# First weights converted by halves, last tokens of a pair stored in one transfer, and a new hand-written order, in an attention and MLP kernel on one core

## The chip, the core and the metric

One NeuronCore of a Trainium2 chip runs the whole program. The metric is the device time of one execution in microseconds (us); smaller is better. TensorE (PE) multiplies matrices, VectorE (DVE), ScalarE (ACT) and GpSimd (POOL) work element by element, and SyncE (SP) issues every transfer (DMA) of this kernel. Each engine takes its own instructions in order.

## The reference, cut to what matters

There are 8 batches (b) of 8 heads, 576 tokens, head size 64, and 32 memories. Softmax weights of `phi` over the tokens compress `k` and `v` to 32 rows per head; each token then attends to these 32 rows; and the result, 4608 tokens by 512 channels, goes through a two-layer MLP with a gate.

```python
a = np.exp(phi - np.max(phi, axis=2, keepdims=True))
a = a / (np.sum(a, axis=2, keepdims=True) + 1e-09)
k_m, v_m = einsum('bhsm,bhsd->bhmd', a, k), einsum('bhsm,bhsd->bhmd', a, v)
attn = softmax(scale * q @ k_m.T)           # over the 32 memories
x = (attn @ v_m) laid out as [4608, 512]
h = x @ w_in                                # 512 x 2048
g = h * np.clip(h + 3.0, 0.0, 6.0) / 6.0
out = g @ w_out                             # 2048 x 512
```

## The kernel before, in words

The program is a list of words, `ORDER`, which `play` turns into instructions one after the other. The order of the words is the order of the instructions on each engine, and the order of the transfers on SP's one queue. Nothing is reordered afterwards; an instruction waits only for its data, for its buffer, and for what stands before it on its engine.

The weights arrive as 64-bit floats and are converted on the chip, once, among the first batches' work. `w_in` comes in 8 units, `w_out` in 8 units too (1 MB each). For a unit u of `w_out` the words are `raw2.u` (load, L189), `ab.1.u` (ACT, size of the number, L198), `cl.1.u` and `sh.1.u` (DVE, clamp and shift, L206 and L209), `ro.1.u` (ACT, the low word, L202), `si.1.u` (DVE, sign, L214), `to.1.u` (DVE, sum, L225), `sx.u` (ACT, high part, L232) and `sy.u` (POOL, low part, L236). The units of `w_in` go the same way under `raw.u.k`, `ab.0.u.k` and so on; their loads, `ab`, `ro`, `si` and `to` are already by halves (k = 0, 1), `cl` and `sh` are whole.

A batch's attention part is `pt` (load of phi), `mx`, `xp`, `tr`, `pc` (exponentials by rows), `kvm.b.t` (memories from five loads `kv.b.t`), `nr`, `nk`, `tp`, `tk`, `sc`, `ct`, `cm`, `cs`, `ex`, `ds`, `dr`, `dm`, `bt`, `bh`, `bl` (the attention weights in two halves of 288 tokens). `fo` multiplies the memories into a unit of `w_in`. A slot is one batch and one tile of 128 of the 2048 channels: `g` (first product, L492), `u`, `m` (gate, L505, L508), `k`, `h`, `l` (parts, L512, L516, L519) and `a` (second product, L528). Batches 0 and 1 go through their slots twice (6 and 8 tiles first, kept in DRAM), the other six once, with 16 tiles each. `wm` (L614) is a product on a constant whose result nobody reads; the order has 60 of them.

Of a batch's 576 tokens, 512 are stored by `store` (L561). The last 64 tokens of two batches (a pair) are gathered and go through `rh`, `rl`, `ra` (L574, L577, L584) together; `re` (L597, L599) writes them to a tile of 128 rows, and `ro2` stores the tile: `rest_store` (L601 to L604) writes rows 0 to 63 behind the first batch of the pair, rows 64 to 127 behind the second. `ro2.3` is the last word of the program.

Of the kernel before, what the change touches and what calls it, by code (L numbers as in the profile page):

```python
# [45 lines left out]

WHOLE = 2
# [10 lines left out]
ct.0.0 kv.1.3 cm.0.0 cs.0.1 fo.0.0 xp.1.1 wm.25 ab.0.1.0 cs.0.0 vh.0.0 ex.0.1 wm.19 wm.22 kv.1.4 wm.7 wm.57 wm.26
wm.48 tr.1.0 wm.31 wm.58 ds.0.1 tr.1.1 raw2.1 wm.36 ex.0.0 xp.1.2 dr.0.1 tr.1.2 pc.1.0 dm.0.1 ds.0.0 wm.39 pc.1.2
wm.40 wm.23 wm.43 ab.0.1.1 kvm.1.0 wm.13 ro.0.1.1 pc.1.1 raw.5.0 kvm.1.1 dr.0.0 kvm.1.2 dm.0.0 cl.0.1 bt.0.1 sh.0.1  # L60
wm.49 ro.0.1.0 g.0.1 kvm.1.3 si.0.1.0 bt.0.0 raw.2.1 kvm.1.4 nr.1 g.0.0 to.0.1.0 si.0.1.1 bh.0.1 nk.1 bl.0.1 g.1.1
wm.24 g.1.0 ab.1.1 to.0.1.1 wm.17 wm.50 wm.42 wm.44 wm.55 cl.1.1 sh.1.1 u.0 ro.1.1 m.0 u.1 q.1.1 si.1.1 h.0 fo.0.1 l.0
wm.21 wm.54 wm.8 wm.0 wm.34 bh.0.0 raw.2.0 vh.0.1 m.1 vl.0.1 k.1 bl.0.0 to.1.1 ab.0.2.0 ab.0.2.1 cl.0.2 a.0.0 sh.0.2
si.0.2.1 raw2.2 tp.1 tk.1 k.0 g.2 raw.3.0 sc.1.1 ro.0.2.1 wm.1 h.1 ro.0.2.0 u.2 ab.1.2 ct.1.1 a.0.1 wm.28 wm.12 g.3
si.0.2.0 to.0.2.0 l.1 q.1.0 cm.1.1 to.0.2.1 u.3 ab.0.3.0 wm.16 a.0.2 m.2 m.3 raw2.3 cl.1.2 ro.1.2 h.2 sx.1 wk.0 l.2
raw.3.1 sh.1.2 wm.47 a.0.3 sc.1.0 cs.1.1 fo.0.2 vh.0.2 sy.1 raw2.4 ex.1.1 ct.1.0 a.1 vl.0.2 wk.1 k.3 ab.0.3.1 cm.1.0
ds.1.1 h.3 cs.1.0 fo.1.0 vh.1.0 k.2 vl.1.0 si.1.2 ro.0.3.1 ro.1.3 pt.2 raw.5.1 to.1.2 g.4 a.2 ex.1.0 cl.0.3 l.3
ab.0.5.0 sx.2 ab.1.3 u.4 ds.1.0 dr.1.0 m.4 g.5 raw2.6 raw.4.0 a.3 u.5 sy.2 h.4 ab.0.5.1 m.5 q.2.1 dr.1.1 h.5 dm.1.0
fo.1.1 dm.1.1 l.4 fo.1.2 ro.0.5.0 bt.1.0 k.5 l.5 a.4 raw2.5 bh.1.0 vh.1.1 vh.1.2 bt.1.1 a.5.0 a.5.1 bl.1.0 bh.1.1
bl.1.1 mx.2 pn.2 vl.1.1 vl.1.2 g.6 sh.0.3 k.4 a.5.2 cl.0.5 si.0.3.0 ro.0.5.1 g.7 e.0.0 ro.0.3.0 u.6 to.0.3.0 m.6 e.0.1  # L70
si.0.3.1 mo.2 eo.0.0 h.6 to.0.3.1 a.5.3 u.7 k.6 raw.4.1 l.6 g.8 a.6.0 ro.1.4 m.7 raw.7.1 g.9 e.0.3 cl.1.3 u.8 sp.2
a.6.1 a.6.2 sh.0.5 e.0.2 m.8 g.10 h.7 k.7 ab.0.4.0 eo.0.1 a.6.3 k.8 l.7 u.9 si.0.5.0 ro.0.4.0 ab.0.4.1 m.9 si.0.5.1
to.0.5.0 raw.6.0 k.9 h.9 cl.0.4 l.9 sh.0.4 si.0.4.1 fo.1.3 a.7 vh.1.3 vl.1.3 u.10 to.0.5.1 h.8 ab.1.4 g.11 l.8 m.10
si.0.4.0 a.8 h.10 u.11 l.10 wk.2 m.11 cl.1.4 g.12 sh.1.3 to.0.4.0 k.10 u.12 ro.1.5 si.1.3 a.9 q.2.0 to.1.3 sh.1.4 wk.5
# [84 lines left out]
def attention_ffn_kernel(ctx: ExitStack, tc: tile.TileContext, pn, pt, kv, kl, qt, w1, w2, out):  # L159
# [547 lines left out]
```

## Time and profile before

| | |
|---|---|
| runs timed | 702.39 us (median of 3; 702.25, 702.39, 703.63) |
| the profiled execution | 701.81 us, of which the profile's span is 699.8 us |
| PE busy | 686.5 us (98% of the span), 5330 matmuls |
| DVE, ACT, POOL busy | 385.2, 325.3, 81.8 us |
| DMA moved | 98.10 MB, mean 140 GB/s |

PE is the engine to look at: what it does not do in its 98% is a little over 13 us, at the two ends for the most part. The other engines matter where PE waits for them. Times inside the profile count from the start of its span.

### The profile page before, as it was taken

The page shows a single profiled execution, that of the slowest core. Times are in us where ns is not written, and L with a number is a line of the kernel's source. Part 1 is how long each engine was busy: PE and PEld are TensorE (multiplying, and loading weights), DVE is VectorE, ACT ScalarE, POOL GpSimd, SP SyncE. Part 2 cuts the span into 40 slices and gives each one's busy share as a digit, 9 for nine tenths or more (in the row PEclk, how much of TensorE's full clock was granted, in tenths as well). Part 3 has the DMA queues.
Part 4 walks back from the last instruction along what each step waited for, and adds up shares of the span by engine and source line. Part 5 has one row for each costly group of instructions (what it writes and reads, how often), then busy time and mean ns, then how long its engine had stood idle before and what let it go on. Part 6 is the DMA issues. An engine that isn't in the chain of part 4 may idle for free. (4 is left out here: it accounts for less than half of the span.)

```text
span 699.8 us, 12717 instructions
## 1 busy us (share of the span) xinstructions
PE 686.5 (98%) x5330; PEld 579.4 (83%) x5330; DVE 385.2 (55%) x596; ACT 325.3 (46%) x635; POOL 81.8 (12%) x60
## 2 busy tenths in 40 slices
PE   6999999999999999999999999999999999999997
PEld 5778878888788888988878887888878888798885
DVE  5999989855744336633555434833355434652331
ACT  5787677545434343643344443544334433363340
POOL 0344020310400004000130001200021000400000
PEclk9999999999999999999999999999999999999999
DMA  9995837243415605540145431514038040410002
GB/s 360 410 417 207 297 119 268 94 140 121 133 61 182 267 1 154 187 166 1 66 159 185 143 122 55 221 62 155 0 145 281 2 151 1 136 61 1 1 0 76
DMA packets 28761, 98.10 MB, mean 140 GB/s; under 512 B 3104, under 2 KB 3872, under 8 KB 27680
## 3 DMA queue, kind: packets, MB, share of 16 engines
q1 hardware_dynamic: 28704, 97.29, 38.4%
q8 instruction: 42, 0.69, 0.4%
q14 instruction: 15, 0.12, 0.0%
HBM read 81.54 MB, written 15.73 MB: 139 GB/s over the span
## 5 line engine op out<-in xcount | busy, mean ns | idle before, releaser
L528 PE MATMUL acc<-w,parts 128*128 128x512 f32 x1536 | 379.0, 392 | 0.1
L528 PEld LDWEIGHTS acc<-w,parts 128*128 128x128 f32 x1536 | 279.6, 188 | 61.1 <-issue 7.7
L508 DVE SCALAR_TENSOR_TENSOR gf<-gf,ph 128x576 f32<-128x576 f32 x128 | 95.4, 751 | 173.4 <-ACT gf L505 172.8
L492 PE MATMUL ph<-phi,both 128*128 128x288 f32 x1008 | 173.1, 293 | 1.0 <-DVE both L471 0.8
L505 ACT ACTIVATE gf<-ph,three 128x576 f32<-128x576 f32 x128 | 94.5, 742 | 171.1 <-PE ph L492 138.3
L492 PEld LDWEIGHTS ph<-phi,both 128*128 128x128 f32 x1008 | 152.2, 188 | 12.3 <-issue 2.1
L519 DVE TENSOR_TENSOR parts<-gf,parts 128x512 fp32r<-128x512 f32 x128 | 90.2, 711 | 40.6 <-ACT parts L516 40.0
L492 PE MATMUL ph<-plo,both 128*128 128x288 f32 x504 | 108.1, 296 | 0.0
L516 ACT CAST parts<-gf 128x512 fp32r<-128x512 f32 x128 | 78.9, 619 | 62.0 <-DVE gf L508 30.6
L492 PEld LDWEIGHTS ph<-plo,both 128*128 128x128 f32 x504 | 80.3, 188 | 0.0
L415 POOL TENSOR_TENSOR st<-st,mx 128x576 f32<-128x576 f32 x15 | 18.3, 1228 | 401.3 <-DVE mx L411 398.4
L471 DVE TENSOR_TENSOR both<-pv,both 128x512 fp32r<-128x512 f32 x63 | 41.6, 680 | 23.2 <-ACT both L467 23.2
L584 PE MATMUL acc<-w,parts 128*128 128x512 f32 x192 | 46.3, 391 | 0.0
L467 ACT CAST both<-pv 128x512 fp32r<-128x512 f32 x63 | 35.5, 589 | 20.9 <-PE pv L454 18.4
L584 PEld LDWEIGHTS acc<-w,parts 128*128 128x128 f32 x192 | 35.6, 188 | 8.0 <-ACT o L550 0.4
L512 ACT COPY rest<-gf 128x64 f32<-128x64 f32 x128 | 30.0, 242 | 18.5 <-DVE gf L508 18.4
L454 PE MATMUL pv<-w,kvT 64*32 64x256 f32 x1024 | 32.5, 380 | 0.9 <-DMA w<-w_kept 0.9
L236 POOL TENSOR_TENSOR w<-tmp,w 128x1024 fp32r<-128x1024 f32 x8 | 20.7, 2583 | 90.7 <-ACT w L232 60.5
L454 PEld LDWEIGHTS pv<-w,kvT 64*32 64x32 f32 x1024 | 18.0, 106 | 12.6 <-issue 3.2
L440 POOL TENSOR_TENSOR plo<-pT,phi 128x576 fp32r<-128x576 f32 x16 | 23.9, 1499 | 15.6 <-ACT phi L435 15.3
L418 ACT ACTIVATE st<-st 128x576 f32<-128x576 f32 x16 | 10.9, 686 | 30.3 <-POOL st L415 30.1
L614 PE MATMUL acc<-rest,ident 128*128 128x128 f32 x120 | 19.7, 301 | 1.6 <-DVE rest L660 1.6
(61 smaller groups left out, 391.9 us busy)
## 6 DMA issues: line engine op xcount, KB each, us to landing
w<-w_kept SPq DMA_DIRECT2D x48, 512.0 KB, 6.3
kvt<-in_kv SPq DMA_DIRECT2D x32, 516.0 KB, 6.8
qh<-in_qt SPq DMA_DIRECT2D x16, 576.0 KB, 10.1
raw<-in_w SPq DMA_DIRECT2D x8, 1024.0 KB, 7.6
raw<-in_w SPq DMA_DIRECT2D x16, 512.0 KB, 9.7
out_t<-o SPq DMA_DIRECT2D x16, 512.0 KB, 3.5
ptile<-in_pt SPq DMA_DIRECT2D x8, 576.0 KB, 4.1
w_kept<-w SPq DMA_DIRECT2D x8, 512.0 KB, 4.3
```

Of the source, the lines that this page charges most:

```text
L440: nc.gpsimd.tensor_tensor(plo, self.pT[hf], probs[self.b, hf][0].bitcast(F32), ALU.subtract)
L454: nc.tensor.matmul(self.pv[u][j * M : (j + 1) * M, g], self.kvT[rows, g, j * M : (j + 1) * M], chunk[rows, j, :].bitcast(F32), start=True, ...
L467: nc.scalar.copy(both[:, 0], self.pv[u])
L471: nc.vector.tensor_tensor(both[:, 1], self.pv[u], both[:, 0].bitcast(F32), ALU.subtract)
L492: nc.tensor.matmul(self.ph[:, hf], w[:, g, fs], x[:, g * HALF : (g + 1) * HALF], start=(i == 0), stop=(i == len(seq) - 1),)
L505: nc.scalar.activation(self.halves(), self.ph, AF.Relu, bias=three)
L508: nc.vector.scalar_tensor_tensor(self.halves(), self.halves(), 6.0, self.ph, ALU.min, ALU.mult)
L512: nc.scalar.copy(rest[:, self.f, at : at + REST], self.gf[:, MAIN:])
L516: nc.scalar.copy(self.parts[:, 0], self.gf[:, :MAIN])
L519: nc.vector.tensor_tensor(self.parts[:, 1], self.gf[:, :MAIN], self.parts[:, 0].bitcast(F32), ALU.subtract)
L528: nc.tensor.matmul(accs[self.run, t], self.parts[:, k, t * P : (t + 1) * P], w, start=self.first and i == 0, stop=self.last and i == 2,)
L584: nc.tensor.matmul(accs["rest", self.p], self.parts[:, i // 2, t * P : (t + 1) * P], w2_parts(4 * self.r + t)[i % 2], start=self.r == 0 an ...
```

## The change

Three things change.

1. `load_w2`, `clamp` and `shift` take a half k, and `w_out` is laid out in DRAM with the two halves of a unit one after the other. For units 0, 1 and 2 each of `raw2`, `ab`, `cl`, `sh`, `ro`, `si` and `to` becomes two words, one for each half. Units 3 to 7 stay whole; their load now reads two runs per partition instead of one.
2. `rest_store` issues one transfer instead of two: `out` is viewed as batches by tokens by channels, and the two batches' last 64 tokens are one pattern of 2 x 64 rows on the DRAM side; on the SBUF side stands the tile of 128 rows. There are four such stores.
3. The first half of `ORDER`, up to about slot 36, is written anew; the later half is the same word for word. The number of `wm` words stays 60.

```diff
-    def load_w2(u):
-        part = wpool.tile([P, UNIT], I64, name=f"raw2_{u}", tag=f"w2_{u}")
-        nc.sync.dma_start(out=part, in_=w2[u])
-        raw[1, u] = {0: (slice(0, UNIT), *words(part))}
+    raw_w2 = {}
+
+    def load_w2(u, k=None):
+        if u not in raw_w2:
+            raw_w2[u] = wpool.tile([P, UNIT], I64, name=f"raw2_{u}", tag=f"w2_{u}")
+        n = UNIT // 2
+        cols = slice(0, UNIT) if k is None else slice(k * n, (k + 1) * n)
+        part = raw_w2[u][:, cols]
+        src = w2[u].rearrange("k p n -> p k n") if k is None else w2[u, k]
+        dst = part.rearrange("p (k n) -> p k n", k=2) if k is None else part
+        nc.sync.dma_start(out=dst, in_=src)
+        raw.setdefault((1, u), {})[k or 0] = (cols, *words(part))
...
-    def clamp(*u):
-        clamped = sizes[u].bitcast(F32)
+    def of_part(u, part):
+        return sizes[u] if part is None else sizes[u][:, raw[u][part][0]]
+
+    def clamp(*u, part=None):
+        clamped = of_part(u, part).bitcast(F32)
         nc.vector.tensor_scalar(clamped, clamped, LOW, TOP, ALU.max, ALU.min)
...
     def rest_store(p):
-        for k in range(2):
-            row = (2 * p + k + 1) * S - REST
-            nc.sync.dma_start(out=out[row : row + REST], in_=outs["rest", p][k * REST : (k + 1) * REST])
+        last = out.rearrange("(b s) d -> b s d", s=S)[2 * p : 2 * p + 2, MAIN:]
+        nc.sync.dma_start(out=last, in_=outs["rest", p])
...
-    w2 = c(w_out.reshape(NFT // 2, 2, P, DM).transpose(0, 2, 1, 3)).reshape(NFT // 2, P, UNIT)
+    w2 = c(w_out.reshape(NFT // 2, 2, P, DM))
```

The start of the two orders, up to the fifth load of batch 0's keys and values:

```
before: pt.0 raw2.0 wm.53 mx.0 xp.0.0 xp.0.2 ab.1.0 tr.0.0 wm.32 wm.9 wm.35 wm.6 pc.0.0 cl.1.0 tr.0.2 kv.0.1 xp.0.1 wm.41
        raw.0.0 wm.45 kv.0.0 tr.0.1 wm.3 sh.1.0 raw.0.1 kv.0.2 kvm.0.0 kvm.0.1 wm.5 pc.0.1 wm.11 wm.30 ro.1.0 kv.0.3 kvm.0.2 ...
after:  pt.0 mx.0 wm.3 wm.58 raw.0.0 xp.0.2 ro.0.0.0 raw2.0.0 raw.0.1 tr.0.2 wm.39 ab.0.0.0 wm.18 wm.59 raw2.0.1 ab.0.0.1
        xp.0.0 ab.1.0.0 cl.0.0 ab.1.0.1 cl.1.0.0 kv.0.0 kv.0.2 ro.1.0.0 wm.36 wm.34 wm.6 wm.57 tr.0.0 pc.0.0 wm.24 wm.14 ...
```

## Rows read from the trace of the kernel before

**Rows 1.** The head of the profile's page and its first part: busy time of each engine, share of the span, instructions.

```profile
span 699.8 us, 12717 instructions
PE 686.5 (98%) x5330; PEld 579.4 (83%) x5330; DVE 385.2 (55%) x596; ACT 325.3 (46%) x635; POOL 81.8 (12%) x60
```

**Rows 2.** Busy time by stretch of the span. After the stretch and its length come PE, weight loads, DVE, ACT and POOL with their instructions, the granted clock of TensorE, the busy share of the DMA engines and GB/s.

```profile
0.00:10.00 10.00, 4.27 (x18) 3.79 (x19) 3.49 (x7) 4.97 (x9) 0.70 (x6) 1.00 0.82 318
10.00:20.00 10.00, 9.28 (x139) 7.27 (x138) 7.75 (x11) 5.94 (x11) 0.97 (x1) 1.00 1.03 414
20.00:60.00 40.00, 39.76 (x393) 30.72 (x385) 37.96 (x58) 32.02 (x57) 15.52 (x10) 1.00 1.02 415
60.00:100.00 40.00, 39.86 (x273) 33.27 (x272) 36.90 (x57) 28.62 (x53) 7.87 (x5) 1.00 0.54 193
100.00:200.00 100.00, 99.34 (x799) 83.82 (x798) 71.29 (x104) 53.61 (x102) 18.25 (x10) 1.00 0.40 133
```

**Rows 3.** The end in order of time: start, length, engine, line, operation; in brackets how long the engine had been idle and what ended that.

```profile
695.63 0.42 DVE L599 TENSOR_SCALAR o<-acc 128x256 f32<-128x256 f32 x1 [2.49 <-ACT o L597]
696.08 1.11 SPq L604 DMA_DIRECT2D out_t<-o x2
```

**Rows 4.** The DMA view of 696 to 700 us, in 40 slices of 0.1 us: GB/s of each slice, then the packets and the issues.

```profile
GB/s 0 0 0 0 0 0 0 0 0 0 0 0 205 287 164 225 205 164 185 205 246 266 143 225 82 21 0 0 0 0 0 0 0 0 0 0 0 0 0 0
DMA packets 160, 0.26 MB, mean 66 GB/s; under 512 B 32, under 2 KB 32, under 8 KB 160
q1 hardware_dynamic: 160, 0.26, 28.4%
out_t<-o SPq DMA_DIRECT2D x2, 128.0 KB
```

**Rows 5.** The DMA view of 683 to 687 us, again in slices of 0.1 us: a store of 512 KB (L561) with rows of 2 KB.

```profile
GB/s 0 0 0 0 0 0 0 0 164 0 0 0 143 287 348 369 430 348 348 328 348 430 389 369 328 369 123 21 20 20 20 20 41 20 20 20 41 20 20 0
out_t<-o SPq DMA_DIRECT2D x1, 512.0 KB
```

**Rows 6.** The DMA view of 685.75 to 686.95 us, the end of the same store.

```profile
DMA packets 15, 0.03 MB, mean 22 GB/s; under 512 B 2, under 2 KB 2, under 8 KB 15
q1 hardware_dynamic: 15, 0.03, 5.8%
```

**Rows 7.** Two small transfers of batch 2 (L295), each of 4 rows of 128 B from 4 partitions to 4 rows in DRAM: their issue in SP's timeline, and the DMA view of 66 to 69 us.

```profile
65.22 1.18 SPq L295 DMA_DIRECT2D nmx<-nmxT x2
DMA packets 17, 0.02 MB, mean 6 GB/s; under 512 B 16, under 2 KB 16, under 8 KB 16
q8 instruction: 1, 0.02, 2.0%
q1 hardware_dynamic: 16, 0.00, 0.3%
```

**Rows 8.** The four pairs of stores by line: the issues with their length (least, median, most), who waited for them (nobody), and the time from issue to landing; and from the timeline the first pair and what ACT then writes to a tile of the same ring.

```profile
L604 SPq DMA_DIRECT2D out_t<-o x8: 472/585/1139, 274.5 to 696.6; - x8
DMA to landing us min/median/max: 4.6/4.8/4.9
274.54 1.88 SPq L604 DMA_DIRECT2D out_t<-o x2
281.59 0.62 ACT L516 CAST parts<-gf 128x512 fp32r<-128x512 f32 x1 [0.69 <-DVE gf L508]
```

**Rows 9.** PE's first instructions in order of time.

```profile
1.60 0.77 PE L614 MATMUL acc<-rest,ident 128*128 128x128 f32 x2 [1.60 <-DVE rest L660]
6.50 1.30 PE L322 MATMUL turns<-ident,ptile 128*128 128x128 f32 x4 [4.13 <-ACT ptile L307]
12.37 0.94 PE L614 MATMUL acc<-rest,ident 128*128 128x128 f32 x6
22.15 1.83 PE L614 MATMUL acc<-rest,ident 128*128 128x128 f32 x14
```

**Rows 10.** Steps of the conversion of weights in the first 80 us, with different shapes apart: count, busy us, mean ns, idle time before.

```profile
L206 DVE TENSOR_SCALAR tmp<-tmp 128x1024 f32<-128x1024 f32 x10 | 6.9, 688 | 2.5 <-ACT tmp L198 2.5
L214 DVE SCALAR_TENSOR_TENSOR tmp<-raw,tmp 128x512 uint32<-128x512 uint32 x10 | 6.8, 681 | 0.1
L225 DVE CUSTOM_DVE_ANT_0 w<-raw,tmp 128x1024 uint16<-128x1024 uint16 x9 | 6.2, 688 | 0.6
L225 DVE CUSTOM_DVE_ANT_0 tmp<-raw,tmp 128x2048 uint16<-128x2048 uint16 x3 | 3.7, 1222 | 1.9 <-ACT raw L202 1.8
L214 DVE SCALAR_TENSOR_TENSOR tmp<-raw,tmp 128x1024 uint32<-128x1024 uint32 x3 | 3.7, 1220 | 0.0
L198 ACT ACTIVATE tmp<-raw 128x512 f32<-128x512 f32 x12 | 7.9, 679 | 0.6 <-DMA raw<-in_w 0.6
L198 ACT ACTIVATE tmp<-raw 128x1024 f32<-128x1024 f32 x4 | 4.6, 1143 | 0.0
```

**Rows 11.** The low parts of `w_out`'s units 0 and 1 on POOL, and the first second products that use them, from the timeline.

```profile
19.03 2.38 POOL L236 TENSOR_TENSOR w<-tmp,w 128x1024 fp32r<-128x1024 f32 x1 [17.72 <-ACT w L232]
48.66 2.67 POOL L236 TENSOR_TENSOR w<-tmp,w 128x1024 fp32r<-128x1024 f32 x1 [1.72 <-ACT w L232]
37.87 0.95 PE L528 MATMUL acc<-w,parts 128*128 128x512 f32 x3
53.17 2.88 PE L528 MATMUL acc<-w,parts 128*128 128x512 f32 x12
```

More of the change, by code (lines that the diff above doesn't have):

```diff
@@ L58 @@
[L58 to L62, printed above, removed]
@@ new lines @@
+xp.1.2 tr.1.0 cs.0.0 wm.7 wm.49 fo.0.0 kv.1.1 kv.1.2 cs.0.1 ab.0.1.1 wm.25 ex.0.1 ex.0.0 cl.0.1 ds.0.1 kv.1.3 dr.0.1
+sh.0.1 wm.19 wm.29 wm.38 vh.0.0 kv.1.4 dm.0.1 ds.0.0 wm.8 wm.51 wm.30 wm.31 wm.17 wm.22 tr.1.2 pc.1.0 wm.11 wm.16
+raw2.1.0 tr.1.1 wm.26 raw2.1.1 kvm.1.0 dr.0.0 pc.1.2 kvm.1.1 si.0.1.0 bt.0.1 raw.2.0 pc.1.1 kvm.1.2 si.0.1.1 dm.0.0
+raw.2.1 bt.0.0 raw.5.0 kvm.1.3 ro.0.1.1 bh.0.1 kvm.1.4 g.0.1 wm.46 g.0.0 wm.23 wm.45 wm.54 wm.28 wm.47 wm.40 ro.0.1.0
+nr.1 to.0.1.0 bl.0.1 raw2.2.1 q.1.1 wm.9 ab.1.1.0 nk.1 ab.1.1.1 wm.44 wm.12 cl.1.1.0 to.0.1.1 u.0 cl.1.1.1 sh.1.1.1
@@ new lines @@
+sx.5 g.19 a.17 l.18 sh.1.6 u.19 k.18 vl.0.6 g.20 ab.1.7 xe.2.1 eo.1.0 m.19 k.19 h.19 cl.1.7 sh.1.7 si.1.6 l.19 to.1.6
+si.1.7 sy.5 fetch.2.3 rc.2.0 rc.2.1 a.18 sx.6 g.21 u.20 m.20 a.19 sy.6 h.20 u.21 kv.2.0 l.20 g.22 to.1.7 m.21 k.20
+u.22 a.20 m.22 h.21 sx.7 k.21 sy.7 l.21 fo.1.6.7 kvm.2.0 kvm.2.1 kvm.2.2 kvm.2.3 kvm.2.4 vh.1.7 vl.1.7 nr.2 a.21 wk.7
+pn.3 h.22 vh.1.6 l.22 nk.2 g.23 wk.6 a.22 u.23 m.23 h.23 l.23 g.24 vl.1.6 a.23.0 k.22 k.23 g.25 u.24 m.24 h.24 k.24
+a.23.1 u.25 l.24 e.2.0 g.26 m.25 e.2.1 a.23.2 g.27 u.26 m.26 k.26 a.23.3 fetch.2.0 eo.2.0 h.26 k.25 e.2.2 kv.3.0
@@ new lines @@
+ra.0.0 rl.0.1 u.34 k.32 rl.0.2 m.34 h.32 l.32 sp.3 g.35 u.35 ra.0.1 m.35 a.31.2 g.36 h.35 a.31.3 l.35 k.35 xa.3.1
+xe.3.1 u.36 kv.3.3 xa.3.0 rc.3.1 kv.3.2 xe.3.0 e.3.3 m.36 xa.3.2 xe.3.2 rh.0.3 ra.0.2 a.32.0 rl.0.3 h.34 kvm.3.0
+kvm.3.1 kvm.3.2 kvm.3.3 kvm.3.4 k.34 e.3.2 l.34 eo.3.1 e.3.1 u.33 eo.3.0 a.32.1 fetch.2.7 nr.3 m.33 kv.4.4 ra.0.3
+fetch.2.4 h.36 fetch.2.6 fetch.2.5 g.37 re.0.0 k.36 h.33 nk.3 l.33 a.32.2 k.33 l.36 u.37 g.38 re.0.1 m.37 a.32.3 u.38
+g.39 k.37 m.38 h.37 l.37 k.38 tp.3 a.33 tk.3 u.39 m.39 fo.2.4.5.6.7 h.38 l.38 a.34 vh.2.4 fetch.3.3 k.39 fetch.3.0
@@ new lines @@
+dm.3.0 vl.3.2 kv.4.3 q.4.0 kv.4.1 bl.3.1 bt.3.0 ro2.0 fetch.3.6 vl.3.1 bh.3.0 vl.3.0 k.46 a.46 vh.3.3 bl.3.0 vl.3.3
+g.48 a.47.0 u.48 g.49 k.47 m.48 h.48 a.47.1 k.48 l.48 u.49 g.50 m.49 h.49 a.47.2 l.49 u.50 g.51 k.49 m.50 e.4.0 xa.4.2
+xa.4.0 a.47.3 u.51 xa.4.1 g.52 h.50 e.4.3 k.50 xe.4.1 l.50 xe.4.0 m.51 a.48.0 xe.4.2 e.4.1 h.51 a.48.1 u.52 eo.4.0
+l.51 kvm.4.0 kvm.4.1 kvm.4.2 kvm.4.3 kvm.4.4 m.52 k.52 e.4.2 k.51 eo.4.1 a.48.2 nr.4 fetch.3.7 nk.4 fetch.3.5 g.53
+h.52 a.48.3 u.53 g.54 m.53 l.52 tp.4 a.49 u.54 m.54 h.54 k.53 l.54 h.53 g.55 tk.4 k.54 a.50 u.55 m.55 l.53
@@ new lines @@
+a.63.0 dm.4.1 fo.4.0.1.2.3 e.5.0 bt.4.1 xa.5.0 a.63.1 vh.4.1 fetch.4.6 bt.4.0 vh.4.0 fetch.4.4 ra.1.0 rh.1.2 kv.5.1
+vl.4.0 kv.5.2 vh.4.3 vl.4.1 vh.4.2 k.62 vl.4.2 bh.4.0 bh.4.1 vl.4.3 a.63.2 bl.4.0 ra.1.1 e.5.2 bl.4.1 rl.1.2 g.64
+a.63.3 u.64 g.65 k.63 xe.5.0 rh.1.3 rl.1.3 ra.1.2 u.65 m.64 e.5.3 h.64 m.65 eo.5.1 q.5.1 l.64 h.65 g.66 kv.5.0 k.64
+a.64.0 u.66 g.67 m.66 k.66 h.66 a.64.1 l.66 ra.1.3 e.5.1 u.67 xa.5.2 eo.5.0 xa.5.1 fetch.4.5 l.65 fetch.4.7 m.67 g.68
+re.1.0 re.1.1 h.67 xe.5.2 k.65 xe.5.1 a.64.2 u.68 g.69 m.68 h.68 a.64.3 k.68 k.67 kvm.5.0 kvm.5.1 kvm.5.2 kvm.5.3
@@ L202, in rounding, with shift @@
         nc.scalar.activation(low, low, AF.Copy, scale=2.0**-29)
-    def clamp(*u):
-        clamped = sizes[u].bitcast(F32)
+    def of_part(u, part):
+        return sizes[u] if part is None else sizes[u][:, raw[u][part][0]]
+    def clamp(*u, part=None):
+        clamped = of_part(u, part).bitcast(F32)
         nc.vector.tensor_scalar(clamped, clamped, LOW, TOP, ALU.max, ALU.min)
-    def shift(*u):
-        nc.vector.tensor_scalar(sizes[u], sizes[u], 3, 0x3FFFFFF8, ALU.logical_shift_left, ALU.bitwise_and)
+    def shift(*u, part=None):
+        size_ = of_part(u, part)
+        nc.vector.tensor_scalar(size_, size_, 3, 0x3FFFFFF8, ALU.logical_shift_left, ALU.bitwise_and)
     def sign(*u, part=0):
@@ L278, in __init__ @@
             self.b = b
-            self.aux = [nc.vector if b == 0 and hf == 0 else nc.gpsimd for hf in range(2)]
+            self.aux = [nc.vector if (b, hf) in ON_VECTOR else nc.gpsimd for hf in range(2)]
             self.st, self.of, self.pT, self.pv, self.psc = {}, {}, {}, {}, {}
@@ L642, in play @@
                 BY_PART[name](*n[:2], part=n[2] if len(n) > 2 else 0)
+            elif name in BY_PIECE:
+                BY_PIECE[name](*n[:2], part=n[2] if len(n) > 2 else None)
             elif name in PLAIN:
```

104 lines of the change are left out of this document (44 added, 60 removed).

## The prediction

> **What bounds the kernel now.** The first view to read is the busy time of each engine. PE is busy for 686.5 of 699.8 us [rows 1], so a change in the order can give back only what PE idles, or take PE's time where it now has none to spare. The second view is busy time by stretch [rows 2]: where the 13 us of idle lie. In the first 10 us PE idles 5.73 us; from 10 to 200 us, the part whose order is rewritten, it idles 0.72 + 0.24 + 0.14 + 0.66 = 1.76 us in all. The third view is the start in order of time [rows 9]: most of the 5.73 us is two waits, 1.60 us for the constants and 4.13 us until ACT has worked on the first load of phi. The fourth is the end [rows 3, 4]: DVE's last step ends at 695.63 + 0.42 = 696.05 us, SP issues the two last stores from 696.08, their data move in 14 slices from 697.2 to 698.6 us, and the span ends at 699.8. No other work stands after 696.05, so the last transfer's own length is kernel time one for one. That is the place to look at, although it is the smallest edit of the diff.
>
> **The last store, now one transfer.** Before, each of the two stores has 64 rows of 2 KB. The packet count tells how many engines share a transfer: 160 packets are 128 rows and 32 packets under 512 B [rows 4], so each store ends with 16 small completion writes, one from each engine. The two small transfers of four rows each are 16 packets on SP's queue in all [rows 7]: 8 rows leave 8 completion writes, 4 for each transfer. A transfer whose pattern begins with four rows ran on four engines. After the change the DRAM side begins with a dimension of 2 (the batches) and only then has 64 rows; the SBUF side has 128 rows. I take it that the store runs on two engines, 64 rows each. The rows don't show a transfer whose two sides begin differently, and this is the largest uncertainty here.
>
> What one engine does alone is in the trace: a store of 512 KB is drained by most engines by 685.75 us, and one engine is left, which moves 15 packets in 1.2 us at 22 GB/s, with 5.8% of 16 engines, so 0.93 of one engine, busy [rows 5, 6]. Two such engines move 262,144 B at 44 GB/s in 5.96 us. Start and end stay as they are: the first data at 697.2 (the first of the two issues stands at 696.08 and the new one takes its place) and 699.8 - 698.6 = 1.2 us behind the last data. So the span would end at 697.2 + 5.96 + 1.2 = 704.36, which is 4.56 us later.
>
> The bounds: in the last stores of before all engines were 28.4% busy over 4 us, 16 x 4 x 0.284 = 18.2 us for 128 rows, so 0.142 us for a row among sixteen busy engines [rows 4]. 64 rows at that price are 9.1 us, and the end moves by 7.7 us. At the other end, the twelve slices in which the lone engine works average 283 / 12 = 23.6 GB/s [rows 5]; two of them need 5.55 us, and the end moves by 4.15. Below all this lies a store on sixteen engines at the 348 to 430 GB/s of the larger store [rows 5]: some 0.73 us for 0.26 MB, and the end comes 0.67 us earlier. I take the lone engine's 22 GB/s, since two engines are nearer to one than to sixteen.
>
> The Trainium skill speaks for this edit on one page and against it on the same: "DMA: Bandwidth & Descriptors", section "Rules for kernel authors", advises one 128-partition transfer in place of two over disjoint halves of the partitions, by which the end would come 0.67 us earlier. Its section "Why a DMA increments its semaphore by 16 and not by 1" says that the engine count is the largest number up to 16 that divides the slowest dimension of both sides; that would be 2 here, and the four engines of [rows 7] agree with it, while no run here shows it for 2.
>
> **The three other pair stores** stand in mid-kernel. They land 4.6 to 4.9 us after the issue, and nobody waited for one [rows 8]. On two engines they land some 4.6 us later. Behind them in SP's queue stand fetches of `w_in` for a later batch, which share the two slow engines; the ring's next tile after the first pair, at 274.54, is written by ACT at 281.59 [rows 8], and five other buffers of that ring are there. I cost them at nothing; if a tile of that ring took the store's slot at once, ACT would wait for 2 to 3 us, at most three times, and PE would lose a part of it. SP's time is free: three issues more early, four fewer later, and no engine waits for SP at the end but through the store itself.
>
> **The halves.** A half costs more than half. On DVE a sign step takes 1220 ns whole and 681 ns by half, a sum 1222 and 688 [rows 10]: 0.14 and 0.15 us more for a unit. Clamp and shift take 688 ns whole; by half they aren't in the trace. They lie between 344 ns and 688; at the sign step's ratio (0.56) it is 384 ns, 0.08 us more for each. So a unit costs DVE about 0.46 us more, three units 1.4 us (0.9 to 5.0 between the bounds). ACT pays 2 x 679 - 1143 = 215 ns for `ab`, and about as much for `ro`: 1.3 us for three units. In 20 to 60 us DVE idles 2.04 us and ACT 7.98 [rows 2], which covers both, DVE's narrowly. What the halves hasten has no hurry: the low part of `w_out`'s unit 0 is done at 19.03 + 2.38 = 21.4 us and first used at 37.87; unit 1 is done at 51.3 and used at 53.17 [rows 11]. So nothing is gained by them on PE's path, and nothing lost while DVE keeps up. The loads come in the same bytes: the DMA engines are full from 10 to 60 us in any order (share 1.02 to 1.03 [rows 2]).
>
> **The new order.** All 60 `wm` and all real products remain, so PE's work is the same and only its idle time can change. Two `wm` instead of one now stand ahead of the first transposes, in the 4.13 us in which PE waits anyway [rows 9]. One `wm` is two matmuls; 14 of them took 1.83 us and 6 took 0.94 [rows 9], so it is worth 2 x 0.11 = 0.22 us. With the 1.76 us of idle that makes 2.0 us, the most that the order can give. The start can't come earlier: `pt.0` and `mx.0` lead in both orders. Against it, the new order puts `kvm.1.3` and `kvm.1.4` and three more `wm` ahead of the first `g`, behind the same loads. I take a third of the cap, 0.7 us, between a gain of 2.0 and a loss of 1.4 (DVE's added time uncovered).
>
> **Sum.** Profiled execution: 701.81 + 4.56 - 0.7 = 705.7 us. The median of the runs is 0.58 above the profiled one; the same sum on 702.39 gives 706.3 us.
>
> **The rivals.**
> 1. *The store still runs on sixteen engines*, because the SBUF side's 128 rows decide. For it: every transfer with 64 or 128 rows does so. Against it: the DRAM side begins with 2. The end comes 0.67 us earlier: 702.39 - 0.67 - 0.7 = 701.0 us, not slower. It decides from the number of completion writes: sixteen and not two.
> 2. *The order takes back all idle time.* 702.39 + 4.56 - 2.0 = 705.0 us. For it: each wait left is short; against it: most of them are issue gaps and landings that any order has.
> 3. *DVE becomes the bound in 20 to 60 us*, where it has 2.04 us to spare. PE then waits for gates and parts: 702.39 + 4.56 + 1.4 = 708.4 us.
> 4. *Two engines are as slow as sixteen together*, 0.142 us a row: 702.39 + 7.7 - 0.7 = 709.4 us.
>
> **How the numbers follow.** The forecast has 0.64, rival 1 0.11, rival 2 0.08, rival 3 0.12, rival 4 0.05. The range leaves out rival 1 and rival 4 (0.16) and reaches from somewhat under rival 2 with the faster lone engine (702.39 + 4.15 - 2.0 = 704.5) to rival 3: 703.6 to 708.8 us. A measurement of this kernel can tell about 0.2% (1.4 us) from no change. Faster by more than that, so under 701.0, is half of rival 1: 0.05. Within it are the other half and a small part of the forecast: 0.08. Slower: 0.87.
>
> **What would show it.** In the last 10 us of the new profile: one issue of 256 KB, a long stretch at 40 to 50 GB/s, two completion writes, and the span's end some 8 us behind the last step of DVE (3.75 now). Sixteen writes and under 1 us of data make rival 1 right. PE's idle from 10 to 200 us tells the order's part: under 1.76 us it gained, over it rival 3 is to be looked for in `m` and `l` on DVE. The prediction is wrong if the store spreads after all, or if a `u`, `h` or `rh` in mid-kernel waits for one of the slow stores.

## The result, and the profile after

The changed kernel takes 708.78 us (median of 708.67, 708.89, 708.67 and 710.21), the kernel before 702.25 to 703.63 us in the same session: a ratio of 1.009, with a 95% interval of 1.0069 to 1.0111, so 4.8 to 7.8 us more. (One execution of before, 3019 us, was disturbed and is left out.) The change makes the kernel slower, as forecast, but by 6.3 us and not by 3.9. The profiled execution takes 708.67 us, its span 706.9 us: 7.1 us more span than before.

Where the 7.1 us lie is read from the end of the timeline of the changed kernel:

```profile
697.76 0.42 DVE L615 TENSOR_SCALAR o<-acc 128x256 f32<-128x256 f32 x1 [2.49 <-ACT o L613]
698.21 0.55 SPq L619 DMA_DIRECT2D out_t<-o x1
```

DVE's last step ends at 698.18 us, 2.13 us later than before [rows 3]; that is all work ahead of the last store. The span ends 706.9 - 698.18 = 8.72 us behind that step, where it was 3.75: the last store costs 4.97 us more. The two sum to 7.1.

The DMA view of 698 to 707 us, in 40 slices of 0.225 us, shows that store:

```profile
GB/s 0 0 0 0 0 0 36 18 18 46 27 55 18 18 55 0 36 55 36 46 55 46 46 55 55 55 46 46 55 55 55 46 46 46 0 0 0 0 0 0
DMA packets 130, 0.26 MB, mean 29 GB/s; under 512 B 2, under 2 KB 2, under 8 KB 130
q1 hardware_dynamic: 130, 0.26, 9.0%
out_t<-o SPq DMA_DIRECT2D x1, 256.0 KB
```

130 packets are 128 rows and two completion writes, where the two stores of before had 32 [rows 4]. The data run from 699.35 to 705.65 us, 6.3 us at 42 GB/s. The Trainium skill, "DMA: Bandwidth & Descriptors", section "Why a DMA increments its semaphore by 16 and not by 1", has it that the engine count is the largest number up to 16 that divides the slowest dimension of both sides; by that rule 2 and 128 give two engines, and the trace agrees with its two completion writes.

The 2.13 us ahead of it are looked for in the busy time by stretch (columns as in [rows 2]). The changed kernel:

```profile
0.00:10.00 10.00, 4.50 (x19) 4.10 (x19) 1.93 (x4) 3.66 (x7) 0.70 (x6) 1.00 0.80 304
10.00:20.00 10.00, 8.68 (x124) 6.75 (x124) 8.72 (x17) 7.38 (x15) 1.08 (x1) 1.00 1.02 413
20.00:60.00 40.00, 39.38 (x398) 29.95 (x398) 38.46 (x67) 31.71 (x61) 15.16 (x10) 1.00 1.01 395
60.00:100.00 40.00, 39.10 (x293) 32.39 (x291) 38.73 (x57) 29.91 (x54) 7.44 (x5) 1.00 0.52 170
100.00:200.00 100.00, 99.61 (x783) 84.52 (x776) 68.71 (x103) 53.30 (x101) 17.06 (x10) 1.00 0.44 146
200.00:300.00 100.00, 99.42 (x814) 84.78 (x813) 48.90 (x82) 42.69 (x88) 7.67 (x6) 1.00 0.44 158
300.00:500.00 200.00, 198.50 (x1532) 169.01 (x1531) 91.88 (x145) 80.90 (x165) 15.23 (x12) 1.00 0.32 115
```

The kernel before, in the two stretches that [rows 2] does not have:

```profile
200.00:300.00 100.00, 100.00 (x818) 85.55 (x817) 49.66 (x83) 43.23 (x90) 7.69 (x6) 1.00 0.44 153
300.00:500.00 200.00, 199.05 (x1535) 169.50 (x1534) 92.78 (x147) 81.22 (x166) 15.25 (x12) 1.00 0.32 114
```

From 10 to 200 us PE now idles 1.32 + 0.62 + 0.90 + 0.39 = 3.23 us; it was 1.76 [rows 2]. Stretch by stretch, PE idles 0.23 us less in the first 10 us, 0.98 more from 10 to 60, 0.76 more from 60 to 100, 0.27 less from 100 to 200, 0.58 more from 200 to 300 and 0.55 more from 300 to 500. That is 2.37 us more idle time, and PE's work is 0.24 us shorter (686.28 us, 686.52 before): the 2.13 us. DVE starts later (1.93 us of work in the first 10 us, 3.49 before) and is then nearly full up to 100 us (38.73 of 40 us from 60 on, 36.90 before). The longest waits of PE over the whole span, but for the two at its start, are these (us in total, times, longest):

```profile
PE pv L470 <- DMA w<-w_kept: 1.4, 1, 1.4
PE pk L372 <- ACT pnat L343: 1.2, 2, 0.8
PE pv L470 <- DVE both L487: 0.9, 1, 0.9
PE ph L508 <- ACT kvn L389: 0.6, 1, 0.6
PE ph L508 <- DVE both L487: 0.5, 2, 0.4
```

The first is a load at 357 us, which took 0.87 us in the profile of before. The second is for ACT at 16 and 29 us, the third for DVE at 62 us, the fourth for ACT at 219 us. Nothing waited for the three slow stores in mid-kernel.

### The profile page after: what moved, and what is told of

The parts are those of the page before. It is cut to its first block, busy times and chain, and to the rows that moved or that the text cites. A ratio compares the mean times of both kernels' runs of the same rounds, so it can differ in the third digit from the quotient of the medians.

```text
span 706.9 us, 12715 instructions
## 1 busy us (share of the span) xinstructions
PE 686.3 (97%) x5330; PEld 578.7 (82%) x5330; DVE 384.5 (54%) x608; ACT 326.5 (46%) x641; POOL 79.9 (11%) x60
## 5 line engine op out<-in xcount | busy, mean ns | idle before, releaser
L535 DVE TENSOR_TENSOR parts<-gf,parts 128x512 fp32r<-128x512 f32 x128 | 88.1, 696 | 43.5 <-ACT parts L532 42.8
L210 ACT ACTIVATE tmp<-raw 128x512 f32<-128x512 f32 (+1 forms) x27 | 20.4, 764 | 3.1 <-DMA raw<-in_w 1.6
```

The lines of the kernel that those rows point to most:

```text
L535: nc.vector.tensor_tensor(self.parts[:, 1], self.gf[:, :MAIN], self.parts[:, 0].bitcast(F32), ALU.subtract)
```

## The experiments

A ratio is that of a run's times to those of the kernel before on the same chip, with its 95% interval; "level" is the median of before there. "Two stores" means that `rest_store` is that of before.

### The parts taken apart

The changed kernel with two stores:

```diff
     def rest_store(p):
-        last = out.rearrange("(b s) d -> b s d", s=S)[2 * p : 2 * p + 2, MAIN:]
-        nc.sync.dma_start(out=last, in_=outs["rest", p])
+        for k in range(2):
+            row = (2 * p + k + 1) * S - REST
+            nc.sync.dma_start(out=out[row : row + REST], in_=outs["rest", p][k * REST : (k + 1) * REST])
```

> The changed kernel with the last tokens of a pair stored by two transfers again, new order and halves kept. Theory (the single store costs about 5.0 us at the end, and the new order with its halves about 2.1 us before it): 708.8 - 5.0 = 703.8 us, some 0.2% over the kernel before, with the span ending some 3.75 us behind VectorE's last step. Rival A (the single store costs nothing, the whole loss is the order's): 708.8 us stays. Rival B (the single store costs all 6.9 us, the late last step is its doing in some way): 702 us, level with before.

Measured: 704.64 us on a level of 702.95, 1.0023 (1.0014 to 1.0031). The theory holds: the store is some 4 us of the 6.3, the order with its halves the rest (1.0 to 2.2 us here). Run twice more, on other occasions, it came out at 1.0052 and 1.0036 (below).

The reverse diff on the kernel before:

> The kernel before with one edit: the last tokens of a pair in one transfer. Theory: the last transfer runs on two engines, so before + 4.6 to 5.0 us, 707.2 to 707.8 us; the span ends 8.3 to 8.7 us behind VectorE's last step and that step stays at 696.05 us. Rival (all sixteen engines): one issue less in the chain, before - 0.7 us, 701.9 us. Rival A of the run above: level with before.

Measured: 707.39 us, 1.0061 (1.0048 to 1.0074): 4.3 us, with the span's end 8.89 us behind DVE's last step. The single store alone does it. That last step began at 696.69 us here, though everything ahead of it is the kernel before, where it began at 695.63: the profiled execution of before was an early one (its folds, `fo`, at 355 us waited 0.87 us for a load, 1.5 us here). So up to about 1 us of the 2.13 between the two profiles can be scatter, and the order's own loss is read from the timed runs.

The order of before with halves and two stores (each word of units 0 to 2 doubled in place: `ab.1.1` becomes `ab.1.1.0 ab.1.1.1`):

> The order of before with each word of the first three units of w_out doubled in place (both halves one behind the other, on every engine), two transfers for the last tokens. Theory (the placing in the new order loses the 2.1 us, the halves as such are hidden): before + 0 to 0.6 us. Rival C (the halves themselves, some 1.4 us more of VectorE, 1.3 us more of ScalarE and three more loads, lose it): before + 1.4 to 2.1 us, with TensorE idle longer from 10 to 100 us.

Measured: 703.45 us, 1.0006 (0.9997 to 1.0014). The halves as such are hidden, or nearly (-0.2 to 1.0 us).

The new order with whole units (the pair merged: `ab.1.1.0 ... ab.1.1.1` becomes `... ab.1.1`), two stores:

> The new order with the first three units of w_out whole again (each pair of half words merged: the load at the first of the two places, every conversion step at the second), two transfers for the last tokens. Theory (placing): before + 1.5 to 2.1 us stay, since every other word stands as in the new order. Rival C (halves): before + 0 to 0.6 us. A time above before + 2.1 us would say that the halves win something that the new order needs.

Measured: 710.1 us, 1.009 (1.0072 to 1.0108), worse by 4.7 us than with halves. Its DVE waits 3.36 us at 19 us for a low word that ACT now makes whole, and PE 2.56 us at 57 us for DVE. With units merged like this the new order loses more. Merging at the later place puts work late, so this run does not price the order by itself, nor does it show that the order needs halves.

### The store's shape

The kernel before, with one store of the same bytes that runs over all engines:

```diff
-            at = self.b % 2 * REST
-            nc.scalar.copy(rest[:, self.f, at : at + REST], self.gf[:, MAIN:])
+            mine = rest[:, self.f].rearrange("p (s k) -> p s k", k=2)[:, :, self.b % 2]
+            nc.scalar.copy(mine, self.gf[:, MAIN:])
...
     def rest_store(p):
-        for k in range(2):
-            row = (2 * p + k + 1) * S - REST
-            nc.sync.dma_start(out=out[row : row + REST], in_=outs["rest", p][k * REST : (k + 1) * REST])
+        last = out.rearrange("(b s) d -> s b d", s=S)[MAIN:, 2 * p : 2 * p + 2]
+        nc.sync.dma_start(out=last, in_=outs["rest", p])
```

> The kernel before with the last tokens of a pair in one transfer of the same 256 KB, but listed token by token: the two batches' last tokens are interleaved in SBUF (a stride of two where the gate's rest is written), and the destination in DRAM is 64 tokens x 2 batches x 512 instead of 2 batches x 64 tokens x 512. Theory (what confines the transfer to two engines is the leading 2 of the destination, not its being one transfer or its size): sixteen completion writes, data over in under 1 us, one issue less than before, so before - 0.5 to 0.7 us, 702.2 us on a level of 702.9. Rival (one transfer of 256 KB is slow as such): before + 4.3 us, as the run of the single store alone.

Measured: 702.88 us, 0.9994 (0.9985 to 1.0003), level with before. Its DMA view of 699 to 703 us, in slices of 0.1 us:

```profile
GB/s 0 0 0 0 0 0 0 0 0 0 0 0 0 0 0 0 143 328 369 451 389 369 369 185 21 0 0 0 0 0 0 0 0 0 0 0 0 0 0 0
DMA packets 144, 0.26 MB, mean 66 GB/s; under 512 B 16, under 2 KB 16, under 8 KB 144
out_t<-o SPq DMA_DIRECT2D x1, 256.0 KB
```

Sixteen completion writes, and the same 256 KB are over in 0.9 us instead of 6.3. Neither the size nor its being one transfer made the store slow: the leading 2 did. The hoped-for gain of 0.5 to 0.7 us is not there, though: the span ends 3.51 us behind DVE's last step, 3.75 before, so merging two stores is worth 0.24 us at most.

The second of the last two stores issued by ACT:

```diff
-            nc.sync.dma_start(out=out[row : row + REST], ...)
+            (nc.scalar if p == 3 and k else nc.sync).dma_start(out=out[row : row + REST], ...)
```

> The kernel before with one edit: the second of the last pair's two transfers is issued by ScalarE's queue instead of SP's, so that it isn't behind the first issue. Theory (the second issue of 0.67 us is in the chain that ends last): before - 0.5 us, 702.4 us. Rival (ScalarE's own issue starts later or is longer, or the landing of the first ends last anyway): level with before, within 0.2 us.

Measured: 703.24 us, 1.0005 (0.9996 to 1.0014). Both issues start at 697.96 us, and the span ends 3.57 us behind DVE's last step. The second issue was worth 0.2 us, not 0.5.

### Where the order loses

Two single waits of the new order mended (two stores in all runs that follow):

```diff
- ... a.3 m.5 fo.1.2 ro.1.4 ... fo.1.1 a.4 ...   g.37 re.0.0 k.36 h.33 nk.3 ...
+ ... a.3 m.5 ro.1.4 ... a.4 fo.1.2 fo.1.1 ...   g.37 nk.3 re.0.0 k.36 h.33 ...
```

> The run with the new order and two transfers, with two places of the order mended: the folds fo.1.2 and fo.1.1 behind a.4 on TensorE (they waited 0.9 us for VectorE at 62 us while a.4 had all it needs but the low part that GpSimd ends then), and nk.3 ahead of re.0.0 on ScalarE (re.0.0 waits 2 us for a store there, and a gemm of TensorE 0.6 us for nk.3 behind it, at 220 us). Theory (single late words lose the time, each of them mendable): 704.6 - 0.9 - 0.6 = 703.1 us, level with before within 0.2%; both waits are gone from TensorE's list. Rival (VectorE, which is busy 38.8 of 40 us from 60 to 100 us, is the bound there): the first wait moves to a later matmul and some 704.0 us or more remain.

Measured: 707.32 us, 1.0056 (1.0033 to 1.0078), single times from 703.44 to 711.46. Both waits are gone from PE's list, and the kernel is slower. So each mend was run alone, and the unmended order beside them.

> The new order with two transfers, and of the two mends only nk.3 ahead of re.0.0 on ScalarE. The two mends together gave before + 4.0 us where 703.1 us was expected; in that profile ScalarE waits 4.4 us from 80 to 85 us for the landing of a store of partial sums, and TensorE 1.9 us behind it. Theory (that loss belongs to the folds that were moved at 62 us, or to the chip, not to this edit): 0.6 us below the run of the new order with two transfers on this chip, some 704.0 us, without the wait for kvn at 220 us.

> The new order with two transfers, and of the two mends only the folds fo.1.2 and fo.1.1 behind a.4. Theory (taking the wait at 62 us away lets what follows reach 80 to 85 us sooner by under a microsecond, and there a store's landing, which is not sooner, is waited for): the wait at 62 us is gone and the time is level with the new order or above it, 704.5 to 707.5 us, with a scatter of several us from run to run that the unmended order has not. Rival (the scatter came with the chip): 703.7 us with a scatter of about 1 us here.

> The run of the new order with two transfers once more, as the level for the two runs beside it on the same chip. Theory: before + 1.6 us, some 704.5 us, scatter 1.2 us as before. If it comes out above 706 us, the loss of the mended orders is the chip's and not their own.

Measured on a level of 702.48: `nk.3` alone 704.11 us, 1.0027 (1.0014 to 1.0041); the folds alone 706.35 us, 1.0054 (1.0042 to 1.0066); the unmended order 705.39 us, 1.0052 (1.0032 to 1.0072). `nk.3` comes out 1.3 us under the unmended order, with intervals that overlap. The folds gain nothing. The scatter that the second expectation gave to them alone is in the unmended order too (704.56 to 709.17 us), so that part of it misses, and so does the third expectation, 1.6 us over before with a scatter of 1.2 us. What became of the wait at 62 us, the rows say: PE in the run with two stores, then PE and ACT in the run with the folds moved.

```profile
62.97 1.32 PE L470 MATMUL pv<-w,kvT 64*32 64x256 f32 x32 [0.91 <-DVE both L487]
```

```profile
68.42 0.79 PE L508 MATMUL ph<-phi,both 128*128 128x288 f32 x4 [0.86 <-DVE both L487]
83.65 1.19 ACT L210 ACTIVATE tmp<-raw 128x1024 f32<-128x1024 f32 x1 [2.81 <-DMA partial<-o]
87.63 0.79 PE L508 MATMUL ph<-phi,both 128*128 128x288 f32 x4 [0.30 <-DVE gf L524]
```

The wait of 0.91 us for DVE's `both` goes from 62.97, and one of 0.86 us for a later `both` comes at 68.42. That later step takes up what the moved folds give, and now begins at 67.67 us, where it began at 67.07; PE's products behind it begin at 68.42, where they began at 68.44. What PE gained by running ahead it has lost there. Then ACT waits 2.81 us for a store of partial sums to land, and PE 0.30 us behind it.

To find the place, the two orders were joined at `u.0`, at 33 us:

> Halves, two transfers; the order of before (each half word in place) up to the first gemm's relu u.0, some 33 us, and all words that are left in the sequence of the new order. Theory (the front loses most: VectorE's first conversion step waits 1.6 us longer for ScalarE, and VectorE has no gap to catch up in until 100 us): before + 0.4 to 1.0 us, first conversion step near 8.1 us. Rival (the waits behind it, at 62 and 220 us, lose it): before + 1.5 us or more.

> The other way round: the new order up to u.0, and the words that are left in the sequence of the order of before (half words in place). Theory (front): before + 1.3 to 2 us, first conversion step near 10 us. Rival (behind it): before + 0.3 to 0.6 us.

Measured on a level of 702.57: 706.47 us, 1.0054 (1.0041 to 1.0068), and 705.81 us, 1.0044 (1.003 to 1.0057). The theory falls in both runs: the first joined order starts as early as before (DVE's first conversion step at 8.02 us) and still loses 3.9 us. The rival's number is met by the first run (1.5 us or more) and not by the second (0.3 to 0.6 us). Both joined orders cost about as much as the new order itself or more (1.0023 to 1.0052), so their times do not tell which half loses. The first one's profile tells a part: PE idles 1.77 us from 20 to 60 us (0.24 before), 0.94 from 60 to 100 and 0.71 from 200 to 300, so the losses of the new order behind 60 us stay with its rest. (Of the second, only the times are read.)

The traces gave the place. DVE at 17 to 21 us in the run with two stores, and GpSimd beside it:

```profile
17.43 0.68 DVE L241 CUSTOM_DVE_ANT_0 w<-raw,tmp 128x1024 uint16<-128x1024 uint16 x1
18.85 2.73 DVE L241 CUSTOM_DVE_ANT_0 w<-raw,tmp 128x1024 uint16<-128x1024 uint16 x1
21.50 1.34 DVE L303 TENSOR_REDUCE nmx<-ptile 128x2 f32<-128x1152 f32 x1
18.68 2.35 POOL L252 TENSOR_TENSOR w<-tmp,w 128x1024 fp32r<-128x1024 f32 x1 [17.38 <-ACT w L248]
```

The same sum step (`to.0.0.1`) takes 2.73 us instead of 0.68, and it is over 0.55 us after GpSimd's step (`sy.0`) ends at 21.03: it stood still until then. The maximum of batch 1 (L303), on which all of batch 1 hangs, begins at 21.50. The profile of before has that sum end at 18.02 + 0.69 = 18.71 us, before GpSimd's 19.03 [rows 11]:

```profile
18.02 0.69 DVE L225 CUSTOM_DVE_ANT_0 w<-raw,tmp 128x1024 uint16<-128x1024 uint16 x1
18.63 1.35 DVE L287 TENSOR_REDUCE nmx<-ptile 128x2 f32<-128x1152 f32 x1
```

In six profiles of the new order (two stores three times, and the mends of 62 and 220 us) the step took 2.25 to 2.78 us. In that of the changed kernel both begin at 18.92, and DVE won:

```profile
18.92 0.67 DVE L241 CUSTOM_DVE_ANT_0 w<-raw,tmp 128x1024 uint16<-128x1024 uint16 x1
18.92 2.90 POOL L252 TENSOR_TENSOR w<-tmp,w 128x1024 fp32r<-128x1024 f32 x1 [17.62 <-ACT w L248]
```

The Trainium skill, "SBUF — State Buffer", section "SBUF: two separate sides", describes a pair of ports that GpSimd shares with those steps of DVE that have two inputs in SBUF or run in a two-port mode, under an exclusive lock: who starts first holds it for the whole instruction. The trace agrees for this step, which has two inputs: 2.73 us where GpSimd was first, and for GpSimd 2.90 us in place of 2.35 where it was not.

The wait of PE for DVE at 62 us, which the changed kernel has too, stands behind another such hold:

```profile
58.63 2.41 POOL L252 TENSOR_TENSOR w<-tmp,w 128x1024 fp32r<-128x1024 f32 x1 [3.11 <-ACT w L248]
59.37 1.70 DVE L438 TENSOR_SCALAR sm<-sm 128x18 f32<-128x18 f32 x1
61.29 0.63 DVE L487 TENSOR_TENSOR both<-pv,both 128x512 fp32r<-128x512 f32 x1
61.97 1.32 PE L470 MATMUL pv<-w,kvT 64*32 64x256 f32 x32 [0.90 <-DVE both L487]
```

DVE's addition to 18 columns, 0.17 us elsewhere, takes 1.70 us and ends with GpSimd's step at 61.04; the `both` for which PE waits comes right behind. The kernel before has the same hold:

```profile
57.26 1.70 DVE L422 TENSOR_SCALAR sm<-sm 128x18 f32<-128x18 f32 x1
```

There no step that PE waits for stands close behind it, and PE idles only 0.14 us from 60 to 100 us [rows 2]. So it is the neighbour that is new at 62 us, not the hold. No run takes this hold away, and what PE would gain by that is not shown.

The mend of the place at 19 us moves one word, so that GpSimd starts later:

```diff
- ... to.1.0.1 sx.0 wm.33 ... nk.0 wm.32 wm.10 tp.0 wm.27 wm.48 tk.0 wm.55 ...
+ ... to.1.0.1 wm.33 ... nk.0 wm.32 wm.10 tp.0 wm.27 wm.48 tk.0 sx.0 wm.55 ...
```

> The new order with two transfers, and sx.0 behind tk.0 on ScalarE (it was ahead of nk.0), so that sy.0 on GpSimd starts some 2 us later, when to.0.0.1 on VectorE is over. Theory (the collision costs VectorE 1.6 to 2.0 us at 19 us and TensorE about 1 us): to.0.0.1 takes 0.68 us, the maximum of batch 1 starts under 19.5 us, and the time falls by 0.7 to 1.0 us against the new order with two transfers (704.6 and 705.4 us in two calls), to some 703.8 to 704.4 us. Rival (the delay is made up by 38 us, or GpSimd then collides with another step of VectorE): 704.6 us or more.

> The same with nk.3 ahead of re.0.0 as well. Theory (the two places add up): 703.2 to 703.6 us, before + 0.1%. Rival: as with nk.3 alone, 704.1 us.

> The new order with two transfers, unmended, a third time. Theory (the collision at 19 us costs it about 0.7 to 1.0 us against the version without it): 1.0025 to 1.0045 of before, and the step to.0.0.1 takes over 2 us in the profile. Rival (the two are the same, and 1.0052 was scatter): 1.0016 or less.

Measured on a level of 703.04: 704.1 us, 1.0016 (1.0007 to 1.0025), and with `nk.3` as well 703.65 us, 1.0014 (1.0005 to 1.0023). In the first of them the step takes 0.67 us, and GpSimd starts at 21.04. The unmended order, a third time, on a level of 702.6: 704.85 us, 1.0036 (1.0022 to 1.005), and the step takes 2.78 us. So the unmended order stands at 1.0023, 1.0036 and 1.0052, and without the collision at 1.0016 and 1.0014: the first mend lies 0.5 to 2.5 us under the unmended order, where 0.7 to 1.0 was expected, and its interval overlaps with the lowest of the three. That the collision is gone is shown by the traces; the times do not fix its price. PE's idle time from 20 to 60 us says more: 0.62 or 0.63 us in the four profiles without the collision (the changed kernel, these two runs and the last run below), 0.91 to 1.42 us in the six with it, so 0.3 to 0.8 us. `nk.3` on top of it gave nothing that can be told. What is left with both mends, 1.0 us (0.4 to 1.6), has an interval that overlaps with that of the halves in the old order (1.0006), and the wait at 62 us is still in it.

### A version that beats both

The longest wait of PE in mid-kernel was in the order all along: four folds (`fo`) at 355 us wait for a load that stands in SP's queue behind a load that waits 37 us and a store that waits 5.5 us.

```diff
- ... a.60 ct.4.1 pt.5 fetch.4.2 ct.4.0 ... mo.5 ex.4.0 a.62 ds.4.1 fetch.4.0 ds.4.0 dr.4.0 sp.5 ...
+ ... a.60 ct.4.1 fetch.4.2 fetch.4.0 pt.5 ct.4.0 ... mo.5 ex.4.0 a.62 ds.4.1 ds.4.0 dr.4.0 sp.5 ...
```

> A version meant to beat both kernels: the kernel before with the store token by token of the run above, and with the two loads fetch.4.2 and fetch.4.0 moved ahead of pt.5 on SP's queue, where they stood behind a load that waits 37 us and a store that waits 5.5 us for VectorE; four folds of TensorE at 355 us wait 0.9 to 1.5 us for the second of them. Theory: that wait goes whole, before - 0.6 - 0.9 to 1.5 us = 700.8 to 701.4 us. Rival (the buffers of these loads come free late, or the loads then collide with others): only the store's part, 702.3 us.

> The kernel before with only the two loads fetch.4.2 and fetch.4.0 moved ahead of pt.5 on SP's queue, two transfers for the last tokens. Theory (of the 1.7 us that the version with both edits won, the wait of the folds at 355 us is 1.2 us and the store's 0.25 us of a shorter end the rest): before - 0.9 to 1.5 us, 701.0 to 701.7 us. Rival (the store token by token carries it): before - 0.3 us or less.

> The same with the two loads fetch.4.2 and fetch.4.0 ahead of pt.5 as well. Theory (the wait at 355 us is independent of the first half of the order): 1.2 to 1.5 us below the run beside it, some 702.0 us, which is not under the 701.0 us that the old order reaches with the same edit. Rival: the new order's halves give something once its collisions are gone, below 701.0 us.

Measured: with the store by token 701.31 us, 0.9976 (0.9967 to 0.9984); the two loads alone 701.02 us, 0.9977 (0.9967 to 0.9986); on the mended new order 702.27 us, 0.9989 (0.998 to 0.9998). The loads carry the gain, 1.6 us, and the store adds nothing that can be told. PE at 355 us before, and with the two loads moved:

```profile
354.86 1.96 PE L454 MATMUL pv<-w,kvT 64*32 64x256 f32 x64 [0.87 <-DMA w<-w_kept]
```

```profile
349.76 5.37 PE L528 MATMUL acc<-w,parts 128*128 128x512 f32 x23
355.06 1.96 PE L454 MATMUL pv<-w,kvT 64*32 64x256 f32 x64
```

The wait is gone. The kernel before with this one edit is faster than both kernels, by 0.2% over the one before, and the new order gives nothing on top of it.

## Why the prediction was wrong in size

The direction was right, and 708.78 us lies at the upper end of the range, but the loss is 6.3 us and not 3.9. Of the two terms of the sum the store's was a little short, and the order's had the wrong sign.

**The last store: right in its mechanism, short by 0.4 us.** The sum had 4.56 us; the end moved by 4.97 in the profile (the single store alone cost 4.3 us in timed runs, 3.4 to 5.2). Lead and tail were as taken: the first data 1.14 us after the issue, the end 1.25 us after the last. The term that was mis-sized is the 5.96 us of data: it took 6.3. In the last 18 slices with data the two engines move 49 GB/s, above the 44 taken from the lone engine; in the ten slices before, 29 GB/s. The two begin unevenly, and the row of one engine that drains a queue could not show a start.

**The order: the step that failed.** The sum had a gain of 0.7 us, a third of PE's idle time, and a loss of at most 1.4. With two stores the new order took 1.6, 2.5 and 3.7 us more than before (1.0023, 1.0036, 1.0052). The step took PE's idle time as what an order can give and DVE's added time as what it can take. It left out that a new order makes new neighbours. In six profiles of it a sum of DVE stands still beside a step of GpSimd, with 0.32 us between the two before, which costs PE 0.3 to 0.8 us. In all of them, the changed kernel's too, the `both` that PE needs stands behind a step that GpSimd holds: 0.76 us more idle time from 60 to 100 us, and no less with the folds moved. And at 219 us PE waits 0.58 us for `nk.3`, a short step of ACT behind a wait of 2.04 us; in the order of before it stood behind one of 2.47 us, and PE did not need it so soon. These prices are read from idle time; no mend of a single place was clear of the scatter of the timed runs. In the profile of the changed kernel DVE's last step is 2.13 us late, and 702.39 + 4.97 + 2.13 = 709.5 us, beside 708.78; with the least of the three losses it is 709.0.

**The halves: right that they stay hidden, too dear on DVE.** DVE's clamp and shift by half take 416 and 422 ns in the changed kernel, not 384:

```profile
L225 DVE TENSOR_SCALAR tmp<-tmp 128x512 uint32<-128x512 uint32 x6 | 2.5, 422 | 0.1
L221 DVE TENSOR_SCALAR tmp<-tmp 128x512 f32<-128x512 f32 x6 | 2.5, 416 | 0.7 <-ACT tmp L210 0.7
```

But the sum adds lengths of single steps, and steps that follow each other overlap in the trace. Two sign halves in the run of the halves alone, and the whole step before:

```profile
9.63 1.28 DVE L231 SCALAR_TENSOR_TENSOR tmp<-raw,tmp 128x512 uint32<-128x512 uint32 x2
9.83 1.23 DVE L214 SCALAR_TENSOR_TENSOR tmp<-raw,tmp 128x1024 uint32<-128x1024 uint32 x1
```

Together they take 0.05 us more, not 0.14, and DVE is busy for 385.7 us in that run, 0.5 us more than before [rows 1], where the sum had 1.4. In time they cost 0.4 us (-0.2 to 1.0).

**The three stores in mid-kernel: right.** Nobody waited for one.

**The rivals.** The first falls by two completion writes, the second by 3.23 us of idle time, the fourth by 4.97 us where 0.142 us a row would be 7.7. The third gave 708.4 us, nearest of all, but by luck: it let DVE's added work come through, which the run of the halves alone did not show. Its place was half right: in the new order PE does wait for DVE, and a wait taken away comes back at the next step.

**What stays open.** The 3 to 4 us that the joined orders lose were not traced to single steps. In the changed kernel's profile the sum at 19 us was not held, and yet its last step is 2.13 us late: 0.75 us ahead of 60 us, with the two waits for ACT at 16 and 29 us as the longest, then 0.76, 0.58 and 0.55 us at 62, 219 and 357 us, less the 0.27 us from 100 to 200 and the 0.24 us of shorter work. The landing at 357 us scatters from run to run (0.87 to 1.5 us in the order of before). Whether the wait at 62 us goes with the hold ahead of it was not tried.

## What to carry to other kernels

Before two stores are merged, look at the first dimension of both sides: a leading dimension of 2 left two engines for 256 KB and cost 4 to 5 us at the end of the kernel, where the same bytes listed token by token took 0.9 us. An order that is written anew is to be read at its new neighbours, above all DVE beside GpSimd and short copies behind waits, and not by PE's idle time alone. A mend is worth what it gives to the end of the kernel: one wait of 0.9 us came back five microseconds later, while two loads moved ahead of a waiting issue gave 1.6 us for nothing.

## What the runs showed of the hardware

A small step of DVE can be held by GpSimd as long as GpSimd's instruction lasts: the addition to 18 columns, which takes 0.17 us elsewhere, took 1.70 us at 59.37 us in the changed kernel and as long at 57.26 us before, and ended with GpSimd's step both times (lines above). What a hold costs is told by the step behind it: PE 0.90 us in the new order, nothing before. The maximum of batch 1 ran beside the same kind of GpSimd step in its usual 1.35 us (18.63 us before, [rows 11] for GpSimd), so not every step of DVE is held.

In one run a wait of PE was followed by a lower clock. With both places mended, PE waited 1.91 us up to 88.54 us, and the stretch behind shows a granted clock of 0.61, so a mix of full and half speed (2.4 and 1.2 GHz). The columns are those of [rows 2]; the clock follows POOL:

```profile
84.00:88.00 4.00, 2.62 (x12) 1.81 (x10) 1.64 (x3) 3.32 (x5) 0.00 (x0) 1.00 0.58 208
88.00:92.00 4.00, 3.46 (x14) 3.37 (x15) 4.00 (x7) 4.00 (x9) 0.00 (x0) 0.61 0.01 4
```

In the run with the store by token PE waited 2.27 us up to 100.42 us, and its clock stayed at 1.00 from 98 to 106 us; what makes the difference is open.
